# Banded attention and a gated feed-forward on one core: which engine adds the later masks, which blocks of attention run two at a time, and which small product resets a bank

## The chip, the cores and the metric

The kernel runs on one core of one Trainium2 chip. The metric is the device time of one execution in microseconds; before the change the median of three runs is 842.04 us (841.5 to 842.22). Less is better.

## The reference, cut to what matters

Eight sequences of 576 tokens, eight heads of 64; the first four heads see a window of the last 32 tokens, the other four every fourth of the last 128. What comes out of the heads goes token by token through a gated feed-forward of width 2048.

```python
scores = scale * np.matmul(q, k.transpose(0, 1, 3, 2))
mask_plain = (rel >= 0) & (rel < window)                                        # 32
mask_dil = (rel >= 0) & (rel < window * dilation) & (rel % dilation == 0)       # 32 * 4, every 4th
scores = np.where(masks[None, :, :, :], scores, -1000000000.0)
attn = np.exp(scores - np.max(scores, axis=-1, keepdims=True))
attn = attn / (np.sum(attn, axis=-1, keepdims=True) + 1e-09)
x = np.matmul(attn, v)              # then by token: 4608 x 512
h = x @ w_in                        # 512 -> 2048
relu6 = np.clip(h + 3.0, 0.0, 6.0)
out = (h * relu6 / 6.0) @ w_out     # 2048 -> 512
```

## The kernel before, in words

**The work and its units.** The attention is cut into 48 trios (`T`): each has the scores of 24 pairs of a query block (32 tokens) and the key block before it and its own (64 columns), all in one PSUM bank of 128 x 384. A *block* (`block`, line 320) is 24 small products for the scores of one trio, alternating with 24 small products for the values of the trio two places behind; each small product is fp32 and shows as two records, each on 64 rows by 32 columns of TensorE. The first 12 trios (`NFIRST`) run at the start, one step at a time, in the order written out by hand in `ORDER` (line 58). The other 36 are spread over the feed-forward by `attend` (line 812), which takes a tuple `bs` of one or two numbers `b`: block `b` has the scores of trio 12 + b and the values of trio 10 + b. Blocks 36 and 37 have values alone.

**The mask.** For a trio that TensorE masks, `block` first writes the mask into the bank by one bf16 product (line 328: lhsT `spread`, 32 rows, with the 32 distinct rows of the mask), and the small products add to it. For the rest, each small product starts its own piece, and VectorE adds the mask on the way to SBUF (`add_mask`, line 242). Before, the first 24 of the later trios are masked by TensorE (`MASKED`), the last 12 by VectorE.

**After the scores.** VectorE finds the largest of each row (line 271) and scales it (272), ScalarE takes the exponentials (280), VectorE turns the blocks over (375, 376) and ScalarE carries the crossing pieces (383). After the values, each row is divided by its sum: either VectorE makes the reciprocals and ScalarE scales in six pieces (`share`, `shares`, lines 285 and 292; the first 16 of the later trios, `SHARED`), or VectorE does all of it (`normalise`, line 301).

**The feed-forward.** Every fp32 factor is split into a high and a low part, and three products stand for one. The 12 chunks of 384 tokens come in two kinds. The first four (`PLAIN`) run as plain products: `gemm1` (lines 536 to 538) into the two `ps_h` banks, the gate (ScalarE 544, VectorE 547), `gemm2` (586 to 588) into three of the six `ps_a` banks. The other eight run as four groups of two chunks in Strassen's manner with seven products in place of eight: in the first half of a group, eight steps `k` of seven products into `ps_x` (745 to 747) with names A11, A22, S4, S2, A12, S1, S3; in the second half, eight steps of seven products into `ps_o` (736). Their weights come through a ring of eight slots from DRAM (`load_sums`, line 670), where the sums of weights have been put before: VectorE and ScalarE make them (`combine`, line 900), `combo_out` (659) and `combo_plain` (650) store them.

**Where a product goes on from another.** A bank of `ps_x` can be seeded: ScalarE copies A11's bank into a second bank (`seed`, line 1055), and A12 adds to it. A product adds only where the bank's columns are marked as written by TensorE. A small product with start=True unmarks the whole bank on its 32 partitions first, and each small product of values, and of scores not masked by TensorE, had start=True (lines 222, 231, 239). So for group 0, steps 0 and 1 (`WIPED`), one bf16 product (line 1066) marks the bank first.

**What sets the order.** For everything after the start, the code makes a list of operations with durations, what they wait for, and what they take and give of four pools (`work` tiles, `w` slots, `ps_h`, `ps_a`). TensorE's order is that in which the code calls; `_in_time` (line 1339) sets the order of VectorE, ScalarE, GpSimd and SyncE by due times, under these durations. Numbers at the top steer it: `SPOTS` (eight places between steps of the plain part where `attend` runs blocks two at a time), `BESIDE_FIRST` (after A11 of which group and step one block runs), `SPARE` (how many `w` slots must be left over when a sum of weights starts), `EARLY` (how long ahead of its due time a plain copy of weights may go), `GAPS` and `LATER` (how many products of the work before are put between the first products of a group).

**The two ways a block stands.** In a spot: mask, block, mask, block, between `gemm2` and `gemm1`. In a group: mask (group 0 only), one block, behind A11 and ahead of the next A22.

Of the kernel before, what the change touches and what calls it, by code (L numbers as in the profile page):

```python
# [19 lines left out]
P = 128  # L20
QB = 32
# [7 lines left out]
NFIRST = 12  # L29
# [8 lines left out]
EVER = 1.0e6  # L38
SLACK = 0.4
SPOTS = (35, 1), (38, 1), (41, 1), (44, 1), (47, 1), (50, 1), (53, 1), (56, 1)  # L40
# [10 lines left out]
BESIDE_SECOND = set()  # L51
# [35 lines left out]
def windowed_attention_ffn(ctx: ExitStack, tc: tile.TileContext, qk, vp, w, mask, out, out_t):  # L87
# [125 lines left out]

    def mm_scores(t, ps, i, u, r, masked):

        x, rows = kqs[t], slice(r * D, (r + 1) * D)
        h = r if t < NFIRST else 1 - r
        n, kb, at = SLOTS * u + i, (SLOTS + 1) * u + i, QB * (2 * (1 - h) + u)
        return nc.tensor.matmul(  # L219
            ps[at : at + QB, 2 * QB * i : 2 * QB * (i + 1)],  # L220
            lhsT=x[rows, KW + QB * n : KW + QB * (n + 1)], rhs=x[rows, QB * kb : QB * (kb + 2)],
            start=not masked, stop=(i == SLOTS - 1 or not masked),
        )
# [10 lines left out]
    def mm_values(t, ps, i, u, r):  # L234

        rows, n, at = slice(r * D, (r + 1) * D), SLOTS * u + i, QB * (2 * (1 - r) + u)
        return nc.tensor.matmul(  # L237
            ps[at : at + QB, i * W : (i + 1) * W],
            lhsT=ats[t][rows, QB * n : QB * (n + 1)], rhs=vs[t][rows, n, :], start=True, stop=True,
        )  # L240
# [79 lines left out]
    def block(ts, tv, pools=()):  # L320
# [4 lines left out]
        masked = ts is not None and ts < NFIRST + MASKED  # L325
        if masked:
            _, kind, part = trios[ts]
            nc.tensor.matmul(ps[:, :CH], lhsT=spread, rhs=mask_sb[:QB, 3 * kind + part], start=True, stop=False)
# [483 lines left out]
    def attend(bs, pools):  # L812
# [12 lines left out]
        for x in names.values():  # L825
            room[x] = room.get(x, 0) + 1
        beat = op(
            "PE", 0.35 + 0.2 * sum(t < NFIRST + MASKED for t in scores) + 0.535 * len(order), do,
# [4 lines left out]
        for ts in scores:  # L833
            if ts < NFIRST + MASKED:
                x = op("DVE", 0.68, lambda ts=ts: scaled_largest(ts), [beat], ahead=EVER)
            else:
                x = op("DVE", 0.55, lambda ts=ts: add_mask(ts), [beat], takes=ONE, gives=[(names[ts], 1)], ahead=EVER)
                released[names[ts]].append(x)
                x = op("DVE", 0.68, lambda ts=ts: scaled_largest(ts), [x], ahead=EVER)
            for i in range(3):  # L840
                holds = not i and ts < NFIRST + MASKED
                x = op(
                    "ACT", 0.54, lambda ts=ts, i=i: exponents(ts, i), [x], takes=ONE if holds else (),
                    gives=[(names[ts], 1)] if i == 2 and ts < NFIRST + MASKED else (), ahead=EVER,
                )
            if ts < NFIRST + MASKED:
                released[names[ts]].append(x)
# [3 lines left out]
        for tv in values:  # L851
            if tv < NFIRST + SHARED:
# [114 lines left out]
    def trios_of(c, kind):  # L967
        return [split[t] for t in split if trios[t][1] == kind and any(token // CH == c for *_, token in spans(t))]
# [136 lines left out]
    def second_products(g):  # L1105
# [46 lines left out]
        def ship(name, after):  # L1152
            def do():
                j, d = HALF_OF[name]
                to = out_t[2 * g + j, HALF * d : HALF * (d + 1), :].rearrange("(b p) x -> p b x", p=P)
                nc.sync.dma_start(out=to, in_=os[name])

            transfer(0.45, 0.75, do, after, gives=SLOT)
# [67 lines left out]
        def ends(p, x, parts):  # L1226
# [14 lines left out]
            else:  # L1241
                last_parts.extend(scaled("21", "x", x, True, parts))
                if parts[-1] == 1:
                    ship("21", last_parts)
# [26 lines left out]
    with tc.manual_schedule(  # L1271
# [36 lines left out]
        for g in range(GROUPS):  # L1308
            firsts = [products_of(g, k) for k in range(PAIRS)]
            seconds = second_products(g)  # L1310
            for k, i in TURNS[:-2]:
# [3 lines left out]
                if (g, k) in BESIDE_FIRST and i == A11:  # L1315
                    attend((b,), (ps_h, ps_h))
                    b += 1
            assert not gaps
            for n, (p, k) in enumerate(RIGHT_TURNS):
# [8 lines left out]
                if (g, p) in BESIDE_SECOND and k == PAIRS - 3:  # L1328
                    attend((b,), (ps_h, ps_h))
                    b += 1  # L1330
# [208 lines left out]
```

## Time and profile before

| | |
|---|---|
| median of three runs | 842.04 us |
| the profiled execution, its own time | 846.16 us |
| span from its first to its last instruction | 844.0 us |
| TensorE busy, matmuls | 828.2 us (98%), 8758 records |
| VectorE, ScalarE, GpSimd busy | 646.7 (77%), 573.7 (68%), 55.5 us (7%) |
| mean granted TensorE clock | 0.99 |
| DMA | 214.70 MB, mean 254 GB/s |

The profiled execution takes 2.2 us more than its span and 4.1 us more than the median; sums below are made in its time and taken off the median. PE is TensorE's matmuls, PEld its weight loads, DVE VectorE, ACT ScalarE, POOL GpSimd, SP SyncE, which issues the DMAs. A row of the timeline gives start, length, engine, line, operation, out<-in and how many; matmuls overlap in it, so what one costs is read from start to start.

### The profile page before, as it was taken

What the parts mean: (1) busy time and instruction counts of PE and PEld (TensorE: products, weight loads), DVE (VectorE), ACT (ScalarE), POOL (GpSimd) and SP (SyncE); (2) the same over time, 40 slices, a digit from 0 to 9 for tenths busy, and PEclk for the clock granted to TensorE, in tenths of its full rate; (3) what the DMA queues carried; (4) which work ended last, traced back from release to release, by engine and by line L of the source; (5) the groups of instructions that cost most, each with busy time, mean ns of one, the idle gap of its engine ahead of it and who ended that gap; (6) DMA issues with size and microseconds to landing.
All of it is one profiled execution on the core that took longest, in us unless ns stands there. A gap on an engine that the chain in (4) does not pass through costs nothing.

```text
span 844.0 us, 22143 instructions
## 1 busy us (share of the span) xinstructions
PE 828.2 (98%) x8758; PEld 776.8 (92%) x8758; DVE 646.7 (77%) x1313; ACT 573.7 (68%) x1400; POOL 55.5 (7%) x114
## 2 busy tenths in 40 slices
PE   7799999999999999999999999999999999999998
PEld 4589999898888889899899999999999999999997
DVE  4799988556677898888898777888677798445983
ACT  3688776334799885789985598855698755445552
POOL 0000000010222211000400001000001000000000
PEclk8799999999999999999999999999999999999999
DMA  8848332343778899899986898977789766996381
GB/s 280 275 134 251 124 122 84 115 152 115 229 233 267 290 345 378 280 391 392 389 295 233 285 347 298 340 249 258 272 313 319 255 228 234 336 368 219 131 293 57
DMA packets 115767, 214.70 MB, mean 254 GB/s; under 512 B 7504, under 2 KB 40272, under 8 KB 115664
## 3 DMA queue, kind: packets, MB, share of 16 engines
q1 hardware_dynamic: 115664, 213.29, 73.1%
q8 instruction: 69, 1.13, 0.5%
q14 instruction: 34, 0.28, 0.1%
HBM read 174.47 MB, written 38.80 MB: 253 GB/s over the span
## 4 chain that ended last, share of the span: by engine, by line
PE 96%; ACT 2%; issue 1%; DVE 1%; DMA 0%; SPq 0%; DVEq 0%
PE ps_o L736 28%; PE ps_x L745 9%; PE ps_x L747 9%; PE ps_x L746 9%; PE ps_h L536 6%; PE ps_h L537 5%; PE ps_h L538 5%; PE ps_o L586 5%; PE ps_o L588 5%; PE ps_o L587 5%; PE ps_b L237 2%; PE ps_a L219 1%; PE ps_a L229 1%; PE ps_b L219 1%; PE ps_a L237 1%; PE ps_a L345 1%
## 5 line engine op out<-in xcount | busy, mean ns | idle before, releaser
L736 PE MATMUL ps_o<-gh,ring 128*128 128x384 f32 x896 | 230.9, 334 | 0.5 <-ACT gh L1195 0.5
L736 PEld LDWEIGHTS ps_o<-gh,ring 128*128 128x128 f32 x896 | 161.9, 188 | 0.8 <-ACT gh L1195 0.8
L736 PE MATMUL ps_o<-gl,ring 128*128 128x384 f32 x448 | 149.9, 335 | 0.3 <-DVE gl L1199 0.2
L1199 DVE TENSOR_TENSOR gl<-g,gh 128x384 fp32r<-128x384 f32 x224 | 116.5, 553 | 28.2 <-ACT gh L1195 26.0
L1195 ACT CAST gh<-g 128x384 fp32r<-128x384 f32 x224 | 104.3, 513 | 27.8 <-PE ps_o L736 20.3
L745 PE MATMUL ps_x<-x,ring 128*128 128x384 f32 x256 | 88.5, 346 | 0.0
L536 PE MATMUL ps_h<-x,wi 128*128 128x384 f32 x256 | 88.3, 345 | 0.0
L537 PE MATMUL ps_h<-x,wi 128*128 128x384 f32 x256 | 86.4, 338 | 0.0
L538 PE MATMUL ps_h<-x,wi 128*128 128x384 f32 x256 | 86.4, 337 | 0.0
L746 PE MATMUL ps_x<-x,ring 128*128 128x384 f32 x256 | 86.2, 337 | 0.0
L747 PE MATMUL ps_x<-x,ring 128*128 128x384 f32 x256 | 86.1, 336 | 0.0
L736 PEld LDWEIGHTS ps_o<-gl,ring 128*128 128x128 f32 x448 | 84.1, 188 | 0.9 <-DVE gl L1199 0.9
L586 PE MATMUL ps_o<-wo,gh 128*128 128x512 f32 x192 | 75.1, 391 | 0.0
L587 PE MATMUL ps_o<-wo,gh 128*128 128x512 f32 x192 | 74.7, 389 | 0.0
L588 PE MATMUL ps_o<-wo,gl 128*128 128x512 f32 x192 | 74.7, 389 | 0.0
L544 ACT ACTIVATE t<-ps_h,three 128x384 f32<-128x384 f32 x64 | 37.0, 582 | 49.8 <-PE ps_h L538 49.0
L747 PE MATMUL ps_x<-cell,ring 128*128 128x384 f32 x192 | 64.8, 338 | 0.0
L746 PE MATMUL ps_x<-cell,ring 128*128 128x384 f32 x192 | 64.7, 337 | 0.0
L745 PE MATMUL ps_x<-cell,ring 128*128 128x384 f32 x192 | 64.7, 337 | 0.0
L1164 DVE TENSOR_TENSOR g<-g 128x768 f32<-128x768 f32 x64 | 60.8, 952 | 0.0
L547 DVE SCALAR_TENSOR_TENSOR t<-t,ps_h 128x384 f32<-128x384 f32 x64 | 35.0, 548 | 29.1 <-ACT t L544 28.7
L1049 DVE TENSOR_TENSOR s<-ps_x,s 128x384 f32<-128x384 f32 x64 | 35.2, 550 | 24.5 <-ACT s L1042 20.4
(114 smaller groups left out, 1765.4 us busy)
## 6 DMA issues: line engine op xcount, KB each, us to landing
ring<-sums SPq DMA_DIRECT2D x112, 512.0 KB, 8.0
ring<-rights SPq DMA_DIRECT2D x112, 512.0 KB, 6.7
st<-in_w SPq DMA_DIRECT2D x32, 512.0 KB, 4.1
kq<-in_qk SPq DMA_DIRECT2D x39, 416.0 KB, 4.8
v<-in_v SPq DMA_DIRECT2D x39, 390.0 KB, 5.8
sums<-wi SPq DMA_DIRECT2D x24, 256.0 KB, 7.1
rights<-wo SPq DMA_DIRECT2D x24, 256.0 KB, 5.4
out<-o SPq DMA_DIRECT2D x16, 384.0 KB, 2.9
```

The source lines that it names most:

```text
L536: nc.tensor.matmul(ph, lhsT=wt(f, 0)[:, ks], rhs=a, start=(kt == 0), stop=False)
L537: nc.tensor.matmul(ph, lhsT=wt(f, 0)[:, ks], rhs=b, start=False, stop=False)
L538: ins = nc.tensor.matmul(ph, lhsT=wt(f, 1)[:, ks], rhs=a, start=False, stop=(kt == NK - 1))
L586: nc.tensor.matmul(po[c][tt], lhsT=gh[:, rows], rhs=wt(f, 2), start=first, stop=False)
L587: nc.tensor.matmul(po[c][tt], lhsT=gh[:, rows], rhs=wt(f, 3), start=False, stop=False)
L588: return nc.tensor.matmul(po[c][tt], lhsT=gl[:, rows], rhs=wt(f, 2), start=False, stop=(f == NF - 1))
L736: nc.tensor.matmul(banks[part][:, :CH], lhsT=right[:, a, cols], rhs=x, start=(start and not i), stop=(i == 2), skip_group_check=True)
L745: nc.tensor.matmul(bank, lhsT=tile_[:, 0, ks], rhs=h[:, kt], start=(start and kt == 0), stop=False, skip_group_check=True)
L746: nc.tensor.matmul(bank, lhsT=tile_[:, 0, ks], rhs=l[:, kt], start=False, stop=False, skip_group_check=True)
L747: nc.tensor.matmul(bank, lhsT=tile_[:, 1, ks], rhs=h[:, kt], start=False, stop=(kt == 1), skip_group_check=True)
L1195: nc.scalar.copy(two[0], gated_tile(g, q, k))
L1199: nc.vector.tensor_tensor(out=two[1], in0=gated_tile(g, q, k), in1=two[0].bitcast(F32), op=ALU.subtract)
```

## The change

- **Masks.** `by_tensor` takes the place of the comparison with `MASKED`: of the later trios, TensorE masks those whose number is in `PE_MASKS` (the 37 in it has no trio, so 15: b = 0, 4, 5, 6, 9, 11, 12, 15, 16, 17, 19, 20, 21, 22, 30); VectorE masks the other 21. For these 15 the mask product has lhsT `ident_b` and all 128 rows of the mask in place of `spread` and 32 rows.
- **Values.** `SHARED` becomes a set; of the trios that exist (b 0 to 35) 8 are in it (9, 10, 11, 12, 26, 31, 32, 33), where 16 were.
- **Blocks in the groups.** `BESIDE` says after A11 of which step how many blocks run. Five entries are 2, twelve are 1; 22 blocks as before. Two at a time take two `ps_h` and two `ps_a` banks.
- **Marks.** Of the six small products of later trios that follow each other on the same 32 partitions, only the first (i == 0) has start=True. `WIPED` is empty.
- **Store.** Of the last output `21` of the last group each half is stored when it is done.
- **Numbers.** `SPARE`, `GAPS` (2 to 3), `LATER` (3 to 2), `EARLY` (100 to 130).

```diff
-SPARE = (1, 1, 1, 1, 1, 1, 1, 1), (1, 1, 1, 1, 1, 1, 1, 1)
+SPARE = ((1, 2, 2, 0, 3, 3, 1, 1), (1, 0, 1, 3, 3, 1, 1, 1))
-GAPS = {(0, 0): 2}
-LATER = 3
+GAPS = {(0, 0): 3}
+LATER = 2
-EARLY = 100.0
-MASKED = 24
-SHARED = 16
-WIPED = {(0, 0), (0, 1)}
-BESIDE_FIRST = {(g, k) for g in range(3) for k in range(8 if not g else 7)}
+EARLY = 130.0
+PE_MASKS = frozenset((0, 4, 5, 6, 9, 11, 12, 15, 16, 17, 19, 20, 21, 22, 30, 37))
+SHARED = frozenset((9, 10, 11, 12, 26, 31, 32, 33, 36))
+WIPED = set()
+BESIDE = {(0, 0): 1, (0, 1): 2, (0, 2): 1, (0, 3): 1, (0, 4): 1, (0, 6): 2, (1, 0): 1, (1, 1): 1, (1, 2): 1, (1, 3): 1, (1, 4): 1, (1, 6): 2, (2, 0): 2, (2, 3): 1, (2, 4): 2, (2, 5): 1, (2, 7): 1}
...
+    def by_tensor(t):
+        return t < NFIRST or t - NFIRST in PE_MASKS
...
-            start=not masked, stop=(i == SLOTS - 1 or not masked),
+            start=(not masked and (i == 0 or t < NFIRST)), stop=(i == SLOTS - 1 or not masked), skip_group_check=(not masked and t >= NFIRST),
...
-            lhsT=ats[t][rows, QB * n : QB * (n + 1)], rhs=vs[t][rows, n, :], start=True, stop=True,
+            lhsT=ats[t][rows, QB * n : QB * (n + 1)], rhs=vs[t][rows, n, :], start=(i == 0), stop=True, skip_group_check=True,
...
-            nc.tensor.matmul(ps[:, :CH], lhsT=spread, rhs=mask_sb[:QB, 3 * kind + part], start=True, stop=False)
+            one, rows = (ident_b, P) if ts >= NFIRST else (spread, QB)
+            nc.tensor.matmul(ps[:, :CH], lhsT=one, rhs=mask_sb[:rows, 3 * kind + part], start=True, stop=False)
...
-            if tv < NFIRST + SHARED:
+            if tv - NFIRST in SHARED:
...
+                if len(parts) == 1:
+                    ship("21", last_parts, slice(parts[0], parts[0] + 1))
+                elif parts[-1] == 1:
                     ship("21", last_parts)
...
-                if (g, k) in BESIDE_FIRST and i == A11:
-                    attend((b,), (ps_h, ps_h))
-                    b += 1
+                if i == A11 and (g, k) in BESIDE:
+                    many = BESIDE[g, k]
+                    attend(tuple(range(b, b + many)), (ps_h, ps_h, ps_a, ps_a))
+                    b += many
```

TensorE in the second spot (blocks 2 and 3), at the seam of the two blocks, before: `mi` is the tile that holds the mask and both matrices it is multiplied by, `kq` queries and keys, `a` the turned exponentials.

```order
L237 MATMUL ps_a<-v,a 32x65
L219 MATMUL ps_b<-kq 32x64
L328 LDWEIGHTS mi
L328 MATMUL ps_a<-mi 128x384
L237 MATMUL ps_a<-v,a 32x65
L219 MATMUL ps_a<-kq 32x64
```

The same seam now.

```order
L239 MATMUL ps_a<-v,a 32x65
L221 MATMUL ps_b<-kq 32x64
L239 MATMUL ps_a<-v,a 32x65
L221 MATMUL ps_a<-kq 32x64
```

The mask of block 3 is gone from TensorE, and so is that of block 2 at the head; the 96 small products of the spot follow each other. Of the 16 masks in the spots 8 are left.

VectorE behind the sixth spot (blocks 10 and 11), before: `mx` is the largest, `z` the sum or its reciprocal, `v` a sum of weights, `t` the gate of a `gemm1`.

```order
L271 TENSOR_REDUCE mx<-ps_b 128x6
L272 TENSOR_SCALAR mx<-mx 128x6
L271 TENSOR_REDUCE mx<-ps_a 128x6
L272 TENSOR_SCALAR mx<-mx 128x6
L288 TENSOR_SCALAR z<-ps_a 128x6
L289 RECIPROCAL z<-z 128x6
L288 TENSOR_SCALAR z<-ps_a 128x6
L289 RECIPROCAL z<-z 128x6
L639 TENSOR_TENSOR v<-v 128x256 x2
L547 SCALAR_TENSOR_TENSOR t<-t,ps_h 128x384
```

The same place now; the gate has line 550.

```order
L247 TENSOR_TENSOR e<-ps_b,mi 128x384
L273 TENSOR_REDUCE mx<-ps_a 128x6
L274 TENSOR_SCALAR mx<-mx 128x6
L273 TENSOR_REDUCE mx<-e 128x6
L274 TENSOR_SCALAR mx<-mx 128x6
L290 TENSOR_SCALAR z<-ps_a 128x6
L291 RECIPROCAL z<-z 128x6
L306 TENSOR_SCALAR z<-ps_a 128x6
L307 RECIPROCAL z<-z 128x6
L309 TENSOR_TENSOR x<-ps_a,z 128x384
L550 SCALAR_TENSOR_TENSOR t<-t,ps_h 128x384
```

One addition of a mask and one division have come to VectorE, and two small sums for a weight have gone from ahead of the gate.

SyncE's queue in the first half of group 0, before: `combo_out` stores sums of weights for the second halves (`rights<-sh`, `rights<-v`) between loads of the ring; the last row holds the 19th to 21st loads of `ring<-sums`.

```order
L666 DMA rights<-sh 128x4x256
L666 DMA rights<-v 128x4x256
L190 DMA kq<-in_qk 128x832
L199 DMA v<-in_v 128x780
L666 DMA rights<-sh 128x4x256
L666 DMA rights<-v 128x4x256
L680 DMA ring<-sums 128x2x512 x3
```

The same stretch now; the 19th and 20th loads are the row of two, the 21st the single one, and 22nd to 28th the row of seven.

```order
L683 DMA ring<-sums 128x2x512 x2
L669 DMA rights<-sh 128x4x256
L669 DMA rights<-v 128x4x256
L669 DMA rights<-sh 128x4x256
L669 DMA rights<-v 128x4x256
L683 DMA ring<-sums 128x2x512
L189 DMA kq<-in_qk 128x832
L198 DMA v<-in_v 128x780
L669 DMA rights<-sh 128x4x256
L669 DMA rights<-v 128x4x256
L683 DMA ring<-sums 128x2x512 x7
```

Three pairs of these stores have moved from ahead of the 19th load of the ring to behind it, and four loads of queries and keys for blocks stand earlier against the stores than they did.

More of the change, by code (lines that the diff above doesn't have):

```diff
@@ L324, in block @@
         pv = bank(*pools[1:]) if tv is not None else None
-        masked = ts is not None and ts < NFIRST + MASKED
+        masked = ts is not None and by_tensor(ts)
         if masked:
             _, kind, part = trios[ts]
-            nc.tensor.matmul(ps[:, :CH], lhsT=spread, rhs=mask_sb[:QB, 3 * kind + part], start=True, stop=False)
+            one, rows = (ident_b, P) if ts >= NFIRST else (spread, QB)
+            nc.tensor.matmul(ps[:, :CH], lhsT=one, rhs=mask_sb[:rows, 3 * kind + part], start=True, stop=False)
         for i, u, r in blocks():
@@ L827, in attend @@
         beat = op(
-            "PE", 0.35 + 0.2 * sum(t < NFIRST + MASKED for t in scores) + 0.535 * len(order), do,
+            "PE", 0.35 + 0.3 * sum(by_tensor(t) for t in scores) + 0.535 * len(order), do,
             [*(x for t in values for x in turned[t]), *(landed_k.get(t) for t in scores), *(landed_v.get(t) for t in values),
@@ L833, in attend @@
         for ts in scores:
-            if ts < NFIRST + MASKED:
+            if by_tensor(ts):
                 x = op("DVE", 0.68, lambda ts=ts: scaled_largest(ts), [beat], ahead=EVER)
@@ L840, in attend @@
             for i in range(3):
-                holds = not i and ts < NFIRST + MASKED
+                holds = not i and by_tensor(ts)
                 x = op(
                     "ACT", 0.54, lambda ts=ts, i=i: exponents(ts, i), [x], takes=ONE if holds else (),
-                    gives=[(names[ts], 1)] if i == 2 and ts < NFIRST + MASKED else (), ahead=EVER,
+                    gives=[(names[ts], 1)] if i == 2 and by_tensor(ts) else (), ahead=EVER,
                 )
-            if ts < NFIRST + MASKED:
+            if by_tensor(ts):
                 released[names[ts]].append(x)
@@ L967, in trios_of @@
     def trios_of(c, kind):
-        return [split[t] for t in split if trios[t][1] == kind and any(token // CH == c for *_, token in spans(t))]
+        return [split[t] for t in range(T) if trios[t][1] == kind and any(token // CH == c for *_, token in spans(t))]
     def fill(g, free_after):
@@ L1150, in seed, with ship @@
             return ops
-        def ship(name, after):
+        def ship(name, after, part=slice(0, 2)):
             def do():
@@ L1155, in do @@
                 to = out_t[2 * g + j, HALF * d : HALF * (d + 1), :].rearrange("(b p) x -> p b x", p=P)
-                nc.sync.dma_start(out=to, in_=os[name])
-            transfer(0.45, 0.75, do, after, gives=SLOT)
+                nc.sync.dma_start(out=to[:, part], in_=os[name][:, part])
+            transfer(0.45, 0.75, do, after, gives=SLOT if part.stop == 2 else ())
         def sum_of(name, to, x, y, alu, after, kk):
@@ L1327, in windowed_attention_ffn @@
                     last_read = dict(used)
-                if (g, p) in BESIDE_SECOND and k == PAIRS - 3:
-                    attend((b,), (ps_h, ps_h))
-                    b += 1
                 if g + 1 < GROUPS and (p, k) == (T2, 0):
```

4 lines of the change are left out of this document (1 added, 3 removed).

## The prediction

> **What bounds the kernel now.** First the page: the span and the chain of work that ended last.
>
> ```profile
> span 844.0 us, 22143 instructions
> PE 96%; ACT 2%; issue 1%; DVE 1%; DMA 0%; SPq 0%; DVEq 0%
> ```
>
> The chain is TensorE nearly from end to end. The waits of TensorE say how much of the rest is waiting:
>
> ```profile
> PE ps_a L219 <- issue: 3.8, 3, 1.5
> PE ps_o L736 <- ACT gh L1195: 0.5, 1, 0.5
> PE ps_o L736 <- DVE gl L1199: 0.2, 1, 0.2
> ```
>
> The first is in the start, which the change leaves as it is. After that only two waits are left, 0.7 us together, at the first products of `ps_o` in group 0. The busy times by stage put a place to this (start, plain part ahead of the spots, spots, group 0, group 1, groups 2 and 3):
>
> ```profile
> 0.00:40.00 40.00, 29.19 (x824) 20.12 (x825) 22.85 (x57) 17.71 (x39) 0.59 (x6) 0.81 0.85 287
> 60.00:196.00 136.00, 136.00 (x739) 123.93 (x738) 105.43 (x202) 80.17 (x148) 3.68 (x7) 1.00 0.44 139
> 196.00:312.00 116.00, 116.00 (x1931) 101.61 (x1930) 91.40 (x214) 96.58 (x314) 25.64 (x47) 1.00 0.78 253
> 340.00:506.00 166.00, 165.24 (x2001) 158.45 (x2000) 139.79 (x294) 133.54 (x344) 12.15 (x25) 1.00 0.93 332
> 506.00:674.00 168.00, 167.96 (x1668) 164.51 (x1669) 132.87 (x270) 125.86 (x302) 8.71 (x23) 1.00 0.82 288
> 674.00:844.00 170.00, 166.05 (x956) 165.73 (x955) 111.54 (x195) 85.38 (x179) 0.00 (x0) 1.00 0.66 233
> ```
>
> Columns: the length, then busy us of PE, PEld, DVE, ACT, POOL, the granted clock, the DMA share. From 60 us on TensorE has no gap worth a name and the full clock. So what leaves TensorE's queue leaves the time, as long as what feeds it keeps up.
>
> **What a block costs TensorE.** The second spot, blocks 2 and 3, start to start:
>
> ```profile
> 211.49 0.39 PE L588 MATMUL ps_o<-wo,gl 128*128 128x512 f32 x1
> 211.81 0.33 PE L328 MATMUL ps_b<-mi 32*128 32x384 bf16 x1
> 212.07 0.24 PE L237 MATMUL ps_a<-v,a 64*32 64x65 f32 x1
> ...
> 213.03 0.22 PE L219 MATMUL ps_b<-kq 64*32 64x64 f32 x1
> 213.18 0.33 PE L328 MATMUL ps_a<-mi 32*128 32x384 bf16 x1
> 213.44 0.24 PE L237 MATMUL ps_a<-v,a 64*32 64x65 f32 x1
> ```
>
> ```profile
> 214.83 0.34 PE L537 MATMUL ps_h<-x,wi 128*128 128x384 f32 x1
> ```
>
> A mask holds the queue 0.26 us (211.81 to 212.07, 213.18 to 213.44), and the mask between the blocks has 0.15 us ahead of it in which the last small products run out (213.03 to 213.18). A block without a mask, in group 1:
>
> ```profile
> 487.06 0.34 PE L746 MATMUL ps_x<-cell,ring 128*128 128x384 f32 x1
> 487.24 0.34 PE L747 MATMUL ps_x<-cell,ring 128*128 128x384 f32 x1
> 487.51 0.24 PE L237 MATMUL ps_b<-v,a 64*32 64x65 f32 x1
> ...
> 487.78 0.27 PE L237 MATMUL ps_b<-v,a 64*32 64x65 f32 x2
> ...
> 488.47 0.22 PE L219 MATMUL ps_b<-kq 64*32 64x64 f32 x1
> 488.61 0.44 PE L745 MATMUL ps_x<-x,ring 128*128 128x384 f32 x1
> 488.89 0.33 PE L746 MATMUL ps_x<-x,ring 128*128 128x384 f32 x1
> ```
>
> A large product takes 0.18 us to the next (487.06 to 487.24), but 0.27 ahead of the block and 0.28 behind it: going in costs 0.09, coming out 0.10, and running out 0.14 (488.47 to 488.61). Between, the small products take 0.96 us, in masked blocks (start=False) as in this one (start=True): 212.07 to 213.03 and 487.51 to 488.47. So the start flag has no price of its own, and the edit of the marks moves TensorE's time only through the masks of the banks it saves. The first 16 of a block's 48 small products take 0.27 us (487.51 to 487.78), the other 32 take 0.69, 21.6 ns each: after a first burst they come at a steady rate.
>
> A full-height bf16 product, which the mask now is, exists in the trace only as the marking of a bank:
>
> ```profile
> 347.63 0.34 PE L747 MATMUL ps_x<-cell,ring 128*128 128x384 f32 x1
> 347.81 0.34 PE L1066 MATMUL ps_x<-mi 128*128 128x384 bf16 x1
> 348.08 0.33 PE L328 MATMUL ps_b<-mi 32*128 32x384 bf16 x1
> ```
>
> It follows a large product with no delay (0.18) and holds the queue 0.27 with the change of shape behind it, 0.09 of which any large product ahead of a block pays. So a full-height mask at a block's head adds about 0.17 where the 32-row one added 0.26: the queue changes shape once and not twice. The Trainium skill (TensorEngine Tiling (Array Packing), Key Properties) says that changing the tiling mode drains TensorE; the trace agrees with 0.09 to 0.15 us for each change.
>
> **The change part by part, on TensorE.**
>
> Masks at a head: eight in the spots before, four now; the four that go give 0.26 each (1.04), the four that stay 0.09 each (0.36). In group 0 eight before; those of blocks 16, 17, 19, 20, 21 and 22 stay (6 x 0.09 = 0.54), those of 18 and 23 go (0.52). Sum 2.46 us.
>
> Masks at a seam: eight in the spots, four of which go (blocks 1, 3, 7, 13). Each gives 0.26 + 0.15, and takes back that the second block no longer starts with a burst: 48 x 21.6 ns = 1.04 against 0.96, so 0.08. 4 x 0.33 = 1.32. The four that stay (5, 9, 11, 15) are full-height between blocks, which no row shows: like the 32-row one (0) if the seam costs the same, 0.10 more if the change of shape behind a block costs what it costs L745. I take 0; bounds 0 and +0.4.
>
> Blocks that now join another in the groups (17 with 18, 22 with 23, 31 with 32, 34 with 35; 29 with 30 has a mask between): the second no longer goes in and the first no longer comes out, 0.09 + 0.10 + 0.14 = 0.33, less 0.08: 4 x 0.25 = 1.00. Blocks 29 and 30 lose 0.33 but gain a seam of 0.15 and a mask of 0.26: +0.08.
>
> Marking of banks: two products gone, 0.18 each (347.63 to 347.81 is what one adds): 0.36.
>
> TensorE: 2.46 + 1.32 + 1.00 - 0.08 + 0.36 = 5.1 us less.
>
> The rule that speaks against the joins: the Trainium skill (TensorE: Matmul & The Clock Gate, Wait — 56ns, not 53.3ns?) has a floor of about 25 ns from start to start of matmuls however small. An estimate from it: 48 x 25 ns = 1.2 us for a block in a stream, and all eight joins would give 0.16 less, 1.3 us in sum. The rows above go below that floor (17 ns in the burst, 21.6 after it), so the trace disagrees, and the sum goes by the rows.
>
> **On VectorE and ScalarE.**
>
> ```profile
> L307 DVE TENSOR_TENSOR x<-ps_a,z 128x384 f32<-128x384 f32 x12 | 6.7, 558 | 0.4
> L245 DVE TENSOR_TENSOR e<-ps_b,mi 128x384 f32<-128x384 f32 x12 | 6.5, 545 | 0.0
> L299 ACT ACTIVATE x<-ps_a,z 128x64 f32<-128x64 f32 x84 | 21.8, 359 | 1.3 <-DVE z L289 1.2
> ```
>
> In the spots eight masks (8 x 0.545) and the divisions of ten trios (0 to 8 and 13: 10 x 0.558) come to VectorE: 9.9 us. That makes 91.4 + 9.9 = 101 of about 113, 90%. ScalarE is relieved there by 10 x 6 pieces, 21.8/84 = 0.26 each, 15.6 of its 96.6. In group 0 two masks and two divisions come, 2.2 us beside 139.8. I cost these at nothing: a gate stands within some eleven rows of a spot's landing in VectorE's order as it did before, and TensorE needs a `ps_h` bank back only two steps (over 4 us) later. If that cover is gone, see the third rival.
>
> **Queues and the end.** `EARLY` and `SPARE` move stores of weights ahead of the ring in SyncE's queue. That matters in group 0, where the DMA queues are full (350 to 420 us):
>
> ```profile
> DMA packets 16076, 27.11 MB, mean 387 GB/s; under 512 B 865, under 2 KB 7009, under 8 KB 16064
> ring<-sums SPq DMA_DIRECT2D x17, 512.0 KB, 9.7
> ```
>
> ```profile
> 376.90 4.28 SPq L680 DMA_DIRECT2D ring<-sums  x3
> ```
>
> ```profile
> 387.23 0.34 PE L745 MATMUL ps_x<-x,ring 128*128 128x384 f32 x1
> ```
>
> The 19th load is issued at 376.90, lands by the median at 386.6, and is used at 387.23: 0.6 us to spare, while TensorE will be there over 3 us earlier. Now three pairs of stores (3 MB, some 8 us at 387 GB/s) stand behind that load, against some of the blocks' loads ahead of it. I cost this at nothing too; its price is the second rival's.
>
> `GAPS` and `LATER` move products of equal cost; what they hide is the seed copy behind A11, and one product (some 1.0 us) still stands between it and S2.
>
> The end: the last scaling, its store, and the span's end.
>
> ```profile
> 840.09 0.49 ACT L1116 ACTIVATE o<-ps_o 128x384 f32<-128x384 f32 x1 [0.55 <-PE ps_o L736]
> 840.60 0.37 SPq L1156 DMA_DIRECT2D out<-o  x1
> ```
>
> 3.4 us from issue to end. The last store is now half of 384 KB; at 387 GB/s half is 0.5 us, and nothing if only the landing's latency counts. I take 0.4.
>
> **The sum.** 5.1 + 0.4 = 5.5 us off. The waits at the start of `ps_o` in group 0 (0.7) may go, since the last block of group 0 ends a step earlier; for new waits in the fuller stages I put 1.0. That leaves 5.2: 846.16 - 5.2 = 841.0 for the profiled execution, and 842.04 - 5.2 = 836.8 us for the median.
>
> **The rivals.**
>
> *The joins give less.* If a block in a stream takes 1.2 us, eight joins give 1.3 less: 838.1. For it: the steady rate is seen over 0.69 us only. Chance 0.14.
>
> *The full-height mask is no cheaper* (the change then does not do what it says for 15 masks): if its shape must be changed ahead of it as well and its weights are not there in time, a head costs 0.37 in place of 0.17 and a seam 0.11 more: 10 x 0.20 + 5 x 0.11 = 2.6, so 839.4. Against it: the rows of L1066. Chance 0.09.
>
> *The DMA queues give back in group 0.* They are full from 350 to 420 us; a stage whose bytes are the same cannot end earlier than they land. TensorE arrives 3 to 4 us earlier, the loads only as far as TensorE itself frees the slots earlier, and from the 22nd load on as much stands ahead as before and more. If the stream does not start earlier, TensorE waits there some 2.5 us: 839.3. For it: 0.6 us to spare at 387.23. Against it: the three pairs of stores that moved. Chance 0.18, a third of it within 0.2%.
>
> *VectorE becomes the bound of a pair of blocks*, and the kernel is slower. Thirteen places (eight spots, five pairs) have up to 2 masks, 2 largest, 2 divisions and 8 turnings on VectorE ahead of gates that free TensorE's banks. If a gate is late by 0.4 us at each, the gain is gone (13 x 0.4 = 5.2); the case decides from 0.55 us. At 0.75 it is 9.8 - 5.2 = 4.6 slower: 846.6. For it: 90% busy in the spots. Against it: the gates stand between the rows of a block in VectorE's order, and ScalarE, on which VectorE waits there, is relieved. Chance 0.07.
>
> **How the numbers follow.** The forecast has 0.52, the rivals 0.14, 0.09, 0.18 and 0.07. About 0.2% (1.7 us, so 840.4) is what a measurement here can tell from no change. Faster: 0.52 + 0.14 + 0.09 + two thirds of 0.18 = 0.87; within: 0.06; slower: 0.07. The range: down to 834.9, if no new wait comes (1.0), the joins run half way to the burst's rate (8 x 0.1) and the last store gives its 0.5; up to 840.6, which holds three rivals and the waits of the fuller DMA case, and leaves out VectorE's and the worst of DMA's.
>
> **What would show it.** In the changed profile: TensorE busy about 5 us less, every spot but the third shorter by 0.2 to 0.6; mask to first small product 0.27 with 128 rows, and no gap at the seams of blocks 2/3, 17/18 and 34/35; no L1066. Wrong, if TensorE's waits after 60 us exceed 2 us in sum: waits on `ring` or `kq` between 350 and 420 would show the DMA case, waits on `t`, `gl` or `e` after spots VectorE's, and 1.2 us for the second of two joined blocks the first.

## The result, and the profile after

The changed kernel takes 850.74 us (median of 6 runs, 849.07 to 854.29) against 842.13 us for the kernel before on the same chip: a ratio of 1.0105, 95% interval 1.0082 to 1.0129. It is slower by some 8.6 us where 5.2 us less were forecast. The profiled execution of the changed kernel took 849.78 us, with a span of 847.9.

TensorE's waits after the start, over 60 to 848 us (what waited, for what; us in total, times, longest):

```profile
PE ps_a L221 <- issue: 6.1, 2, 4.4
PE ps_b L239 <- DMA v<-in_v: 2.4, 1, 2.4
PE ps_a L239 <- DMA v<-in_v: 1.4, 1, 1.4
```

Before, the same stretch held 0.7 us of waiting at `ps_o`; those waits are gone, and 9.9 us of others have come. The largest has no engine and no DMA as its releaser: "issue". It stands inside the pairs of blocks 22/23 and 34/35, inside the second block:

```profile
392.80 0.22 PE L221 MATMUL ps_a<-kq 64*32 64x64 f32 x1
392.82 0.22 PE L239 MATMUL ps_a<-v,a 64*32 64x65 f32 x1
397.44 0.26 PE L221 MATMUL ps_a<-kq 64*32 64x64 f32 x1 [4.40 <-issue]
397.44 0.31 PE L239 MATMUL ps_a<-v,a 64*32 64x65 f32 x1
```

```profile
635.89 0.21 PE L221 MATMUL ps_a<-kq 64*32 64x64 f32 x1 [1.71 <-issue]
```

Nothing that the program orders separates the product of 392.82 from that of 397.44: the products on both sides of the stall go into the same banks and come from the same tiles. And after the stall the products last 0.31 in place of 0.22. Busy time by stretch shows what that costs (length, busy us of PE, PEld, DVE, ACT, POOL, granted clock, DMA share, GB/s), first before, then after:

```profile
380.00:400.00 20.00, 20.00 (x293) 18.97 (x292) 17.32 (x45) 18.69 (x53) 1.87 (x3) 1.00 1.05 392
400.00:420.00 20.00, 19.24 (x196) 17.83 (x194) 16.79 (x34) 19.14 (x48) 8.76 (x19) 1.00 1.05 389
```

```profile
380.00:400.00 20.00, 15.60 (x262) 14.95 (x261) 12.73 (x30) 13.59 (x33) 1.52 (x3) 0.91 1.06 392
400.00:420.00 20.00, 20.00 (x108) 20.00 (x107) 15.77 (x33) 17.23 (x41) 5.02 (x12) 0.92 0.95 351
```

The trace has the clock at half for 6.83 us from 396.4, so some 2.9 us of work are lost behind the stall of 4.6. The other two waits are at the first value product of a block, just behind its mask, block 12 in the spots and block 19 in group 0:

```profile
284.51 0.34 PE L331 MATMUL ps_b<-mi 128*128 128x384 bf16 x1
286.23 0.21 PE L239 MATMUL ps_a<-v,a 64*32 64x65 f32 x1 [1.39 <-DMA v<-in_v]
```

```profile
354.22 0.34 PE L331 MATMUL ps_b<-mi 128*128 128x384 bf16 x1
356.93 0.21 PE L239 MATMUL ps_b<-v,a 64*32 64x65 f32 x1 [2.37 <-DMA v<-in_v]
```

Waits 9.9 and clock 2.9 make 12.8 us; less the 5.1 and 0.4 that were forecast for TensorE and the end, and the 0.7 of old waits, that is 6.6 slower. From the first small product of the plain part (74.08 before, 72.15 after) to the end of the span the traces have 769.9 and 775.8: 5.9 slower. The start, which the change hardly touches, differs from one execution to the next: in the profiled ones shown here that product starts at 70.6 to 74.1. Before's was the latest, so the medians lie further apart than the two profiles.

### The profile page after: what moved, and what is told of

It is laid out like the page before. It is cut to its first block, busy times and chain, and to the rows that moved or that the text cites. A ratio compares the mean times of both kernels' runs of the same rounds, so it can differ in the third digit from the quotient of the medians.

```text
span 847.9 us, 22108 instructions
## 1 busy us (share of the span) xinstructions
PE 824.8 (97%) x8747; PEld 778.1 (92%) x8747; DVE 654.7 (77%) x1330; ACT 565.4 (67%) x1352; POOL 59.7 (7%) x114
## 3 DMA queue, kind: packets, MB, share of 16 engines
q8 instruction: 69, 1.13, 0.5%
## 4 chain that ended last, share of the span: by engine, by line
PE 94%; DMA 2%; DVE 1%; issue 1%; ACT 1%; SPq 0%
PE ps_o L739 27%; PE ps_x L748 10%; PE ps_x L749 9%; PE ps_x L750 9%; PE ps_h L539 5%; PE ps_o L589 5%; PE ps_h L541 5%; PE ps_h L540 5%; PE ps_o L590 5%; PE ps_o L591 5%; PE ps_a L221 2%; PE ps_a L239 2%; PE ps_b L239 2%; DMA v<-in_v 1%; PE ps_b L221 1%
## 5 line engine op out<-in xcount | busy, mean ns | idle before, releaser
L386 ACT COPY a<-a_t 32x192 f32<-32x192 f32 x144 | 50.5, 350 | 8.6 <-DVE a L379 5.9
```

## Experiments

**The theory.** TensorE's instructions come by DMA, in packets. The page of the changed kernel has them as a queue of their own (packets, MB, share of 16 engines):

```profile
q8 instruction: 69, 1.13, 0.5%
```

1.13 MB by 69 is 16.4 KB a packet. TensorE has 17,755 records in this trace (products, weight loads and semaphore instructions), some 257 to a packet. Counted in order of start, the stalls stand at fixed places, 256 records apart: number 10177 is 39 x 256 + 193, number 15041 is 58 x 256 + 193. The waits called "issue" in the start of before stand at 705, 961, 1217 and 1473: 193 past 2, 3, 4 and 5 x 256. Each time TensorE goes on 1.3 to 1.5 us after a packet has come in. A block is 24 + 24 small products, each of two records with a weight load each: 192 instructions, gone in 1.04 us (5.4 ns each). A pair is 384, so a whole packet of 256 can lie inside a pair and be used up in 1.4 us. The next one is not there long ahead: over the whole trace of the changed kernel a packet lands between 3.0 us before and 5.0 us after the first record of the packet ahead of it starts. Whether a whole packet does lie inside a pair depends on the place of the boundary: in the changed kernel they are at 115 and 371 of pair 22/23 and at 54 and 310 of pair 34/35; the three other pairs and every spot of two whole blocks have a single one, at 187 to 239.

The rivals: VectorE's gates or PSUM banks freed too late (the forecast's fourth), full DMA queues that delay the ring (its third), and, for the waits on `v`, either the pairs or the stores of weights that were moved up.

In the table, the ratio is to runs of the kernel before on the same chip (843 to 844 us), with its interval.

| Kernel | us | ratio (95%) |
|---|---|---|
| changed, one block a step | 849.02 | 1.0060 (1.0037-1.0082) |
| before, with the pairs | 853.34 | 1.0109 (1.0081-1.0137) |
| changed, 41 more products | 846.27 | 1.0041 (1.0023-1.0059) |
| changed, old stores | 859.28 | 1.0174 (1.0146-1.0202) |
| heads, marks, end alone | 840.27 | 0.9964 (0.9949-0.9978) |
| changed, one block, old stores and gaps | 841.85 | 0.9983 (0.9969-0.9998) |
| VectorE's masks in the spots | 842.82 | 0.9999 (0.9983-1.0015) |
| before, dense stretches | 884.28 | 1.0489 (1.0460-1.0517) |
| changed, one block, old stores | 842.77 | 0.9990 (0.9972-1.0007) |
| changed, 41 more, 18 apart | 851.23 | 1.0085 (1.0056-1.0115) |
| heads, with moved stores | 846.78 | 1.0018 (1.0000-1.0036) |

### Supply of instructions

**The pairs alone, in the kernel before.** `BESIDE` of the changed kernel with its call of `attend`, nothing else:

```diff
-                if (g, k) in BESIDE_FIRST and i == A11:
-                    attend((b,), (ps_h, ps_h))
-                    b += 1
+                if i == A11 and (g, k) in BESIDE:
+                    many = BESIDE[g, k]
+                    attend(tuple(range(b, b + many)), (ps_h, ps_h, ps_a, ps_a))
+                    b += many
```

> The kernel before with one part of the change alone: the blocks of the groups stand in the steps of the changed kernel, five of them in pairs; masks, marks, stores and the end are those of before. Counted in TensorE's stream, the pairs 22/23 and 34/35 hold two packet boundaries each (at about 98 and 354, and at 37 and 293 of their 386 instructions), the other three pairs one. If instruction supply sets the stalls, TensorE stands still inside those two pairs, 3 to 5 us and about 2 us, and nowhere inside the other three; with the lower clock behind the first and the wait at block 19 the kernel takes about 850 (847 to 853). If the pairs only save changes of shape, as forecast, 841.

853.3 us, 9.4 more than before. The stalls came at the two pairs named and nowhere else, with VectorE's work and the stores as before:

```profile
PE ps_a L218 <- issue: 5.6, 2, 4.3
PE ps_x L744 <- DMA ring<-sums: 2.1, 2, 1.7
```

```profile
398.82 0.26 PE L218 MATMUL ps_a<-kq 64*32 64x64 f32 x1 [4.30 <-issue]
```

The 2.1 us for the ring, ahead of the stall, were not in the expectation: a piece of the third rival. The wait at block 19, which was in it, did not come, though the pair 17/18 stands ahead of that block here too. Its load of values goes out ahead of the stores of weights, lands at 353.18 and is used at 355.58. The row of that load here, and then the same load with what stands just ahead of it in the changed kernel, where it lands at 356.80:

```profile
346.60 0.43 SPq L198 DMA_DIRECT2D v<-in_v  x1
```

```profile
347.07 1.30 SPq L669 DMA_DIRECT2D rights<-v  x1
348.47 1.31 SPq L189 DMA_DIRECT2D kq<-in_qk  x1
349.83 1.53 SPq L198 DMA_DIRECT2D v<-in_v  x1
```

So the pair alone does not make block 19 wait; it takes what stands ahead of the load in SyncE's queue as well.

**The boundaries moved.** 41 products of block 16 once more, 164 instructions ahead of the pairs:

```diff
+MORE = 41
+        if ts == NFIRST + 16:
+            for n in range(MORE):
+                mm_values(tv, pv, 0, n // 2 % 2, n % 2)
```

> The changed kernel with 41 small value products of block 16 issued once more (their results are written over by the same products), which puts 164 more instructions into TensorE's stream ahead of the pairs and changes nothing else. The packet boundaries then fall 164 instructions earlier in every pair. If instruction supply sets the stalls, they move: the pairs 22/23 (boundary now at about 207 instead of 115 and 371) and 34/35 (about 146 instead of 54 and 310) have at most some 0.8 us left, and the pairs 29/30 (23 and 279) and 31/32 (31 and 287), which had none, get one each of 1.5 to 4 us, 17/18 (75 and 331) at most 1. If the stalls come from a bank, a gate or a load, which the 41 products do not move, they stay at 22/23 and 34/35 with 4.6 and 1.9 us. The time alone does not tell the two apart: 846 to 852 by either.

846.3 us. Pair 22/23 now runs through, from its mask to the large product behind it in 2.45 us:

```profile
394.14 0.34 PE L332 MATMUL ps_b<-mi 128*128 128x384 bf16 x1
...
396.59 0.44 PE L752 MATMUL ps_x<-x,ring 128*128 128x384 f32 x1
```

and the long stall has moved to pair 17/18, which had none:

```profile
351.00 0.21 PE L222 MATMUL ps_a<-kq 64*32 64x64 f32 x1 [4.10 <-issue]
```

So 164 cheap instructions, 10 to 60 us ahead, move the stall from one pair to another; no bank, gate or load of the pair was touched. That decides it against the first two rivals. The sizes were poorly expected: at 17/18 at most 1 us was expected and 4.3 came, at 29/30 and 31/32 1.5 to 4 were expected and none and 0.6 came. At 34/35, 0.7 us were left, just behind the pair, as expected. What was missed is when the packet arrives. These rows are worked out from the trace's records of packets (times in us; "record" is the first of a new packet, "begun" the time of the record 256 ahead of it):

```
kernel           record  begun   packet in   stalled from  goes on   after packet
changed          10177   391.41  396.13      392.82        397.44    1.31
changed          15041   632.58  634.61      633.96        635.89    1.28
before + pairs   10177   392.59  397.30      394.30        398.82    1.52
before + pairs   15041   633.76  635.21      635.11        636.68    1.47
41 more, 17/18    8897   345.31  349.54      346.69        351.00    1.46
41 more, 29/30   12993   520.25  520.42      no stall      521.96    1.54
41 more, 31/32   14273   596.93  597.53      598.26        598.88    1.35
```

At 345 to 396 us, where the DMA queues are full, the packet was in 4.2 to 4.7 us after the first instruction of the packet before it; with the 1.3 to 1.5 behind it that is some 6 us, and the pair has 1.4. At 520 and 597 it was in after 0.2 and 0.6 us. That is not the length of a fetch: these packets' own transfers took 1.0 to 1.1 us and had started before that first instruction ran. In both, the boundary stands only 23 and 31 instructions into the pair, in the others 37 to 115. So a packet is on its way early where slow, large products stand ahead of the boundary: over the traces of the changed kernel, of the one with 41 more products and of the dense stretches its transfer starts 0.6 us before that first instruction (median) where at most 5 of the 63 records ahead of it are of small products, and 1.5 us after it where 30 or more are. These rows do not part what the place of the boundary does from what the full queues do; the next run does.

**The price by itself.** In the kernel before, 192 products issued once more ahead of blocks 2, 21 and 35:

```diff
+MORE = 192
+        if ts in (NFIRST + 2, NFIRST + 21, NFIRST + 35):
+            for n in range(MORE):
+                mm_values(tv, pv, 0, n // 2 % 2, n % 2)
```

> The kernel before with 192 value products issued once more (768 TensorE instructions, same result) ahead of three blocks: 2 (spots, 213 us, DMA share 0.59), 21 (group 0, 384 us, share 1.05) and 35 (group 2, 631 us, share 0.91). Each makes a stretch of some 960 instructions of 5.4 ns, in which three packet boundaries follow one another. If the supply of instructions is the limit, TensorE stands still at each of these boundaries, and from one to the next it takes what the fetch takes and not 256 x 5.4 ns = 1.4 us: some 3 to 4 us in the spots, 5.5 to 6.5 in group 0, 3 to 4.5 in group 2, so 20 to 30 us slower than before in all. If instructions come fast enough and the stalls in the pairs were something else, the three stretches run through at 1.4 us a packet: some 13 us slower.

41 us slower. All nine boundaries stall, six in one group of TensorE's waits and three in the other:

```profile
PE ps_b L238 <- issue: 13.9, 6, 3.7
PE ps_a L238 <- issue: 4.1, 3, 1.4
```

From boundary to boundary it took 3.36, 3.45 and 3.29 us in the spots, 5.76, 6.20 and 4.00 in group 0, 3.66, 4.02 and 3.91 in group 2. The time was under-expected: in group 0 the clock fell to half for 3.41 and 6.83 us, which the expectation had left out. In group 2 the DMA share while TensorE stalled was 0.01:

```profile
661.00:672.00 11.00, 5.34 (x342) 4.77 (x330) 0.15 (x1) 0.80 (x3) 0.00 (x0) 1.00 0.01 3
```

so 3.3 to 4.0 us for 256 instructions is the rate with quiet queues, not the price of contention; with full ones it was 5.8 to 6.2. The three steps of group 0, one behind the other, show both:

```profile
394.60:400.40 5.80, 2.12 (x149) 1.95 (x139) 0.12 (x1) 2.23 (x6) 0.51 (x1) 1.00 1.05 401
400.40:406.60 6.20, 3.45 (x132) 3.22 (x133) 0.00 (x0) 0.00 (x0) 0.00 (x0) 0.72 0.89 327
406.60:410.60 4.00, 2.15 (x133) 1.90 (x135) 0.00 (x0) 0.00 (x0) 0.00 (x0) 0.61 0.02 6
```

In the third the DMA share has fallen to 0.02, and the step is back to 4.0.

### Loads of the values

**One block a step.**

```diff
-BESIDE = {(0, 0): 1, (0, 1): 2, (0, 2): 1, (0, 3): 1, (0, 4): 1, (0, 6): 2, (1, 0): 1, (1, 1): 1, (1, 2): 1, (1, 3): 1, (1, 4): 1, (1, 6): 2, (2, 0): 2, (2, 3): 1, (2, 4): 2, (2, 5): 1, (2, 7): 1}
+BESIDE = {(g, k): 1 for g in range(3) for k in range(8 if not g else 7)}
```

> The changed kernel, but with one block a step in the groups, as before: the five joined pairs are gone, everything else of the change stays. If the loss comes from the pairs (a packet of 256 TensorE instructions that lies wholly inside a pair is used up in 1.4 us while the next one takes up to 6 us to come, and block 19 follows block 17 by one step), the stalls of 4.6 and 1.9 us, the 2.4 us at the lower clock behind the first and the 2.65 us at block 19 go and the 1.0 us that the joins gave goes too: 850.7 - 11.6 + 1.0 = 840, a little faster than before (ratio about 0.998). If the loss comes from the work moved to VectorE or from the stores that were moved up, all of that is still in this kernel: 850 or more.

849.0 us: near the 850 or more of the second case, which names two causes; the runs below show that it is the stores. The stalls inside pairs and the wait at block 19 are gone, but other waits have grown:

```profile
PE ps_a L239 <- DMA v<-in_v: 6.3, 1, 6.3
PE ps_o L739 <- ACT gh L1198: 1.8, 2, 1.3
PE ps_o L739 <- DMA ring<-rights: 0.4, 1, 0.4
PE ps_o L739 <- DVE gl L1202: 0.3, 2, 0.2
```

The first is block 12's again, 6.3 us, with 6.83 us of half clock from 288.1 us on. So the pairs are not the whole loss, and a second cause was hidden under the first.

**Old stores, pairs kept.** `EARLY = 100.0`, `SPARE` all 1:

> The changed kernel with the order of the weight stores as before (EARLY 100, SPARE all 1). If late loads behind the stores that were moved up made the wait of 1.4 us ahead of block 12 in the spots, that wait goes, and the loads have more to spare; the stalls inside the pairs 22/23 and 34/35 stay within about 1 us of 4.6 and 1.9: 848 to 850. If the full DMA queues of the moved stores are what makes those stalls, they go with them: about 842.

859.3 us, missed by both. Block 12 does not wait, as expected; the stalls inside pairs stay (3.7 and 1.9), so the moved stores do not make them. But block 19's load is later (2.9), the first products of `ps_o` wait 3.3 for ScalarE's `gh`, and the clock falls four times. The pairs with the old order of stores are worse than with the new one.

**One block a step, old stores.** The same two lines in the run with one block a step:

> The changed kernel with one block a step and the stores of weights in the order of before; the gaps and late products stay as changed. It parts the two edits that separated the run with single blocks (6 us slower at block 12's load, 849.0) from the one that had also the old stores and gaps (841.9). If the stores that were moved up are what delays the load, block 12 does not wait and the time is that of the latter, 840 to 844. If the gaps made the difference, 848 to 850.

842.8 us: without the moved stores the 6.3 us at block 12 are gone. With the gaps of before as well it was 841.9:

> The changed kernel with one block a step and with the stores of weights, the gaps and the late products in the order of before: what is left of the change is the sharing of the masks, the divisions, the full-height masks, the marks and the end. If the 6.5 us ahead of block 12 in the run with single blocks came from the stores that were moved up, the load of v for block 10's values lands in time here and that wait is gone; with the pairs gone too the kernel is then faster than before, by up to 5.1 - 1.0 + 0.4 = 4.5 us less the waits at ps_o at 410 to 420 us (0 to 5 us with the clock that they cost): 840 to 844 against 843.9, ratio 0.995 to 1.0. If VectorE's and ScalarE's added work bounds the spots or group 0, waits on e, gh or gl stand there and the ratio is 1.003 or more.

Here ratio 0.9983, inside what was expected. The waits left are in group 0, for the ring (2.2) and for `gl` and `gh` (0.5), and 0.6 in the spots at `ps_h` for ScalarE's `e`:

```profile
PE ps_o L739 <- DMA ring<-rights: 1.6, 1, 1.6
PE ps_h L539 <- ACT e L282: 0.6, 1, 0.6
PE ps_x L748 <- DMA ring<-sums: 0.6, 1, 0.6
```

**The moved stores alone**, on the fastest version (below):

```diff
-EARLY = 100.0
+EARLY = 130.0
-SPARE = (1, 1, 1, 1, 1, 1, 1, 1), (1, 1, 1, 1, 1, 1, 1, 1)
+SPARE = ((1, 2, 2, 0, 3, 3, 1, 1), (1, 0, 1, 3, 3, 1, 1, 1))
```

> The run with the heads alone (840.3, ratio 0.996) with one part of the change added: stores of weights moved up (EARLY 130, the changed SPARE). If the moved stores by themselves delay the loads of the blocks, TensorE waits 1.5 to 6.5 us for v at block 12 and the ratio is 0.999 to 1.005; other waits for ring or kq in group 0 should be no larger. If they harm only beside VectorE's masks, the time stays at 840.

846.8 us in place of 840.3, by one wait:

```profile
291.61 0.28 PE L239 MATMUL ps_a<-v,a 64*32 64x65 f32 x1 [5.40 <-DMA v<-in_v]
```

SyncE's queue shows why, first without the moved stores, then with them (start, us, what is issued):

```profile
271.85 1.69 SPq L189 DMA_DIRECT2D kq<-in_qk  x2
273.59 0.93 SPq L198 DMA_DIRECT2D v<-in_v  x2
```

```profile
266.62 13.99 SPq L660 DMA_DIRECT2D rights<-wo  x15
280.71 0.55 SPq L897 DMA_DIRECT2D out<-o  x1
281.30 1.86 SPq L660 DMA_DIRECT2D rights<-wo  x3
283.27 1.22 SPq L897 DMA_DIRECT2D out<-o  x2
284.58 1.30 SPq L189 DMA_DIRECT2D kq<-in_qk  x2
285.93 0.96 SPq L198 DMA_DIRECT2D v<-in_v  x2
```

Eighteen plain stores stand in the queue ahead of the load for block 12's values, which goes out 12 us later than without them. In the changed kernel it goes out at 280.52 and the wait is 1.4.

**Block 18 in a step of its own**, with the 41 products, so that the pair 17/18 is gone:

```diff
-(0, 1): 2, (0, 2): 1, (0, 3): 1, (0, 4): 1, (0, 6): 2
+(0, 1): 1, (0, 2): 1, (0, 3): 1, (0, 4): 1, (0, 5): 1, (0, 6): 2
```

> The changed kernel with the 41 extra products of block 16 and with block 18 in a step of its own, so that the four pairs left have their packet boundaries at about 207 (22/23), 23 and 279 (29/30), 31 and 287 (31/32) and 146 (34/35). The shift alone left stalls of 4.3 us at pair 17/18 and under 1.1 us at the other pairs. If those 4.3 us and 1.7 us of clock behind them belong to that pair alone, they go: 846.3 - 6.0 + 0.25 = 840.5, ratio 0.997 (843.1 before), though the 41 products cost some 1 us and block 12 still waits 1.4 to 1.7 for its load. If block 18 apart makes TensorE wait for loads in group 0 or at ps_o instead, 844 or more.

851.2 us: a miss, on the side that the last sentence names. No stall of supply is left above 0.7 us, but the pair 22/23, now one step behind block 21, waits twice for values:

```profile
PE ps_a L240 <- DMA v<-in_v: 7.6, 2, 6.3
PE ps_b L240 <- DMA v<-in_v: 0.9, 1, 0.9
```

The 7.6 holds block 12's 1.3 and 6.3 in the second block of the pair. The load of a block's values is issued when the values two blocks before have been used. With one block a step that is two steps, 17.7 us; behind or inside a pair it is one, 8.9 us, and in group 0 a load took 7.0 us to land (349.83 to 356.80 for block 19 in the changed kernel) after what stands ahead of it in SyncE's queue. Block 19's 2.4 us in the changed kernel are of the same kind.

### What of the change gains

**Heads, marks and end alone.** Full-height masks, no marking products, last store in halves; all 24 masks on TensorE, one block a step, all else as before:

```diff
-PE_MASKS = frozenset((0, 4, 5, 6, 9, 11, 12, 15, 16, 17, 19, 20, 21, 22, 30, 37))
-SHARED = frozenset((9, 10, 11, 12, 26, 31, 32, 33, 36))
+PE_MASKS = frozenset(range(24))
+SHARED = frozenset(range(16))
```

with `BESIDE`, `SPARE`, `EARLY`, `GAPS` and `LATER` of before.

> Only the parts of the change that touch TensorE's price for a block and the end: masks of full height, first of six products alone clears the bits (so no marking products), last store in halves. All 24 masks stay on TensorE, one block a step, the divisions, the stores of weights and the gaps as before. By the forecast's own terms: 16 heads x 0.17 = 2.7, marks 0.36, end 0.4, seams 0: 3.5 us faster than before (ratio 0.996), if these terms were sized rightly and nothing waits for it. If group 0 gives back what it gains at the first products of ps_o (ScalarE is busy there), 1.2 us of it go: ratio 0.997. If the full-height mask is no cheaper, 0.999.

840.3 us, ratio 0.9964 (0.9949 to 0.9978): faster than both kernels, and after the start TensorE waits for nothing at all. The expectation mistook a term: 0.17 is what a full-height mask still adds, and the forecast has 0.09 saved at each head. Measured: a spot goes from 15.33 to 15.23 us from start to start (0.10 for a head and a seam), a step of group 0 from 8.90 to 8.81 (0.09). By these it is 16 x 0.09 = 1.4, marks 0.36, the end 0 to 0.65, and the old waits 0.7: 2.5 to 3.2, as measured (3.0).

**VectorE's masks in the spots added**, its eight masks and the divisions:

> As the run with heads alone (full-height masks, marks, end; old stores; single blocks), but in the spots the eight masks and the six divisions of the changed kernel are VectorE's; group 0 is left to TensorE with all its masks. By the forecast's terms 1.3 us for four seams and 0.36 for four heads on top of the heads alone, 5.2 us faster than before: ratio 0.994. If VectorE is late in the spots, TensorE waits there on ps_h (on e or t) 1 us or more in sum and the ratio is that of the heads alone or above it.

842.8 us: no gain over before, and 2.5 us lost against the heads alone. The spots of blocks 0 to 11 take 90.3 us against 90.9 with the heads alone, 0.6 less and not the 1.5 of the forecast's terms (3 x 0.17 and 3 x 0.33). Of the 0.9 that is missing, 0.6 is a wait for a `ps_h` bank on ScalarE's `e`; the rest is not accounted for. In the profiled execution, at 846.6 us the longest of its twelve, group 0 gives back more than that, with 2.5 us for a load of values, 3.41 us of half clock behind it, and 1.2 us for `gh`:

```profile
PE ps_b L239 <- DMA v<-in_v: 2.5, 1, 2.5
PE ps_o L739 <- ACT gh L1198: 1.2, 2, 0.8
PE ps_h L539 <- ACT e L282: 0.6, 1, 0.6
```

## Why the prediction was wrong

**What held.** TensorE's prices. The spots of blocks 0 to 11 were to gain 3 x 0.09 + 3 x 0.26 + 3 x 0.33 = 2.04 and took 1.95 less (91.39 to 89.44 from the first small product of the first spot to that of the seventh, with block 12's wait taken off). A joined pair gives more than the 0.25 forecast. Pair 31/32, in the changed kernel:

```profile
600.31 0.34 PE L739 MATMUL ps_o<-gh,ring 128*128 128x384 f32 x1
...
602.62 0.44 PE L748 MATMUL ps_x<-x,ring 128*128 128x384 f32 x1
```

2.31 from large product to large product. Less the large product itself and with the 0.10 that it pays behind, the pair costs 2.31 - 0.18 + 0.10 = 2.23; two single blocks (487.24 to 488.61 in before) cost 2 x (1.37 - 0.18 + 0.10) = 2.58. So a join is worth 0.35. The first rival, a floor of 25 ns, is out; so is the second, that full-height masks are no cheaper. The end gave 0.65 in nine of the ten kernels with halves (3.06 in place of 3.71 from the last product to TensorE's next instruction) and nothing in one, against 0.4.

**The step that failed.** "From 60 us on TensorE has no gap worth a name and the full clock. So what leaves TensorE's queue leaves the time, as long as what feeds it keeps up." What feeds it was taken to be data. The sum has no term for the instructions themselves, and the joins, 1.00 us of gain, cost 6.5 us of stall and some 2.9 of clock. The profile of before had the sign: "PE ps_a L219 <- issue: 3.8, 3, 1.5", read as a matter of the start, "which the change leaves as it is". Ahead of each of these waits some 232 to 246 of 256 records are of small products: block upon block with little that is large between, which is what the change makes of the groups. The steady rate was measured inside one block of 192 instructions; that says nothing of 384. The Trainium skill (Runtime: NRT & Kernel Launch, Instruction fetch mechanics) states the blocks of 256 instructions, 16 KiB each, and that the next page is fetched while the current one runs; the traces agree, with packets of 16.4 KB and with stalls only at records 193 past a multiple of 256. It also says that the crossing costs little, because instructions are dispatched slower than they are fetched; here the trace disagrees: 1.4 us to use 256 up, 3.3 to 6.2 from one packet to the next.

**The second step that failed.** "`EARLY` and `SPARE` move stores of weights ahead of the ring in SyncE's queue. That matters in group 0." It mattered at block 12, in the spots: the loads of the blocks stand in the same queue, and only the ring's slack was read. The forecast put "some of the blocks' loads ahead of it" but did not ask what stood ahead of the blocks' loads. Measured: 1.4 us in the changed kernel, 5.4 with the moved stores alone.

**The third.** For a pair the forecast counted changes of shape, and not that the values two blocks back are then one step back. Block 19 waited 2.4 us. The pair leaves its load one step in place of two, and what stands ahead of the load in SyncE's queue uses that up: with the pairs alone in the kernel before it did not wait.

**The forecast's rivals.** The third, the DMA queues, named waits "on `ring` or `kq` between 350 and 420"; in the changed kernel there were none. They come up in other kernels: 2.2 us with one block a step and the old stores, 2.1 us ahead of the stall in the kernel before with the pairs, none with the heads alone. So it is real, but was not what decided. The fourth, VectorE, was to make every gate late; no such wait appears in the changed kernel. Four others wait 0.6 us in the spots for a bank that ScalarE's `e` frees, and several 0.2 to 3.3 us for `gh` or `gl` at `ps_o`. It named the right sign and the wrong cause.

**What stays open.** How long a block's load takes behind a given queue (block 12 waits 1.4 us in one order and 6.3 in another with the same two lines of numbers; its load goes out at 280.52 in the one, at 283.69 in the other) was read, not derived. Nor is it known which idle stretch below 2.5 us brings the half clock. And why the wait of 0.7 us at `ps_o` is gone in the version with heads alone was not tried apart; the planner's costs for a mask differ there from before.

## What to carry to other kernels

Before joining short instructions into longer runs, count them: a run that swallows a whole packet of 256 instructions (here with their weight loads) in less than the fetch takes, 3.3 us in quiet and some 6 with full DMA queues on this kernel, stalls however ready its data are, and whether it does can hang on how many instructions stand ahead. A wait called "issue" at equal distances in the record count is the sign. And when a queue is reordered, look up the slack of everything that is issued behind what moves, and when blocks are grouped, count the distance of their loads in time and not in blocks.

## What the runs showed of the hardware

In all thirteen traces TensorE went on 1.2 to 1.5 us after a packet of instructions had landed wherever it had waited with "issue" as the cause, and it did so only at records 193 past a multiple of 256. After 60 us, every idle stretch of 2.5 to 6.3 us (eleven, in nine kernels) brought 3.41 or 6.83 us at half clock. Of the shorter ones, 2.37 (changed), 2.00 and 2.08 (dense stretches) did not, but one of 1.68 (old stores) and one of 1.30 (one block a step) did. The Trainium skill (TensorE: Matmul & The Clock Gate, Part 1: The HAM clock gate) puts the window at 3413 ns, free-running; the traces agree with both: half clock lasted 3.41 or twice that, and within each of the thirteen traces all changes of the clock stand whole multiples of 3.413 us apart (with the old stores those at 358.97, 399.93, 420.41 and 645.69 are 12, 6 and 66 apart). That the idle time within one such window decides alone, they do not show: 1.30 us in one window brought the half clock (one block a step, 411.0 to 414.4), 1.76 in another did not (dense stretches, 663.5 to 666.9). A stall of 4.3 to 4.6 us cost 6 to 7.5 with its clock.
